# First batch's queries in runs of 256, 128 and 384 tokens, and cluster products of both halves in one run

## The chip, the cores and the metric

The kernel runs on one core of one Trainium2 chip. The metric is the device time of one execution in microseconds (us); the time of a kernel is the median of its runs. A profile is one further execution, taken by the hardware profiler. Engines are named as the profile names them: PE (matrix products), PEld (its weight loads, which run beside the products), DVE (vector), ACT (activation functions), POOL and SP. SP computes nothing here; it issues DMAs. POOL casts, and issues DMAs on a software queue. Each engine works through its own instructions in order.

## The reference

Each query and key is given to the cluster of its head whose normalised centroid it fits best; a query attends only to keys of its own cluster. The result goes, token by token, through a gated feed forward.

```python
q_assign = np.argmax(np.einsum('bhsd,hcd->bhsc', q_n, c_n), axis=-1)
k_assign = np.argmax(np.einsum('bhsd,hcd->bhsc', k_n, c_n), axis=-1)
mask = q_assign[:, :, :, None] == k_assign[:, :, None, :]
scores = np.where(mask, scale * np.matmul(q, k.transpose(0, 1, 3, 2)), -1000000000.0)
attn = softmax(scores)                      # over the keys
x = (attn @ v).transpose(0, 2, 1, 3).reshape(B * S, H * D)
out = (1 / (1 + np.exp(-(x @ w_gate))) * (x @ w_val)) @ w_out
```

There are B = 4 batches, H = 8 heads, S = 768 tokens, D = 64; 16 clusters for each head; w_gate and w_val are 512 x 1536, w_out is 1536 x 512.

## The kernel before, in words

**Tiles.** Heads are worked in four pairs p = 0 to 3; `even` and `odd` hold the keys and queries of one pair for the even and the odd tokens, cast to 16 bits, with 16 more rows that mark the cluster ("mask rows"), so that one product gives score and mask at once. For the first batch the mask rows of `even` and of most of `odd` are made by DVE (L506, called from `place`, L675); the rows of the odd queries come by a DMA, `odd<-even` (L693). A block is (batch, half of the tokens qb, pair p) with 384 queries. `attend` (L905) works two of a block's 12 units (head of the pair, 128 keys) at a time: two score products of 384 columns into one `sc` buffer (L921), one exponential over both, 768 columns, into `es` (L939), six value products of 65 columns from `es` (L967). After the twelfth unit DVE divides by the sums (L1005, L1008), and the block is turned into the columns of `x`, by a DMA transpose on SP (L1031) or, where that would be late, by PE and a DVE copy (L1016, L1027): in the before, for pairs 2 and 3 of the first half of batch 0, and for the last block.

**Feed forward.** `feed` (L1055) starts when all four pairs of a half are in `x`: for each of 12 chunks of the hidden layer four gate products and four value products of 384 columns (L1066), a tanh on ACT (L1082), a gated product on DVE (L1093) into `hT`. Then for each 128 tokens three runs of four output products of 512 columns (L1113), a copy by ACT (L1128) and a DMA of 256 KB to the output.

**Preparation.** Pairs of batch 0 are prepared by `prepare_first` and `prepare_pair` (PE transposes L824 and L716, cluster products L870 and L756). Later batches are prepared two pairs at a time by `prepare` (L511): for batch 1's pairs 0 and 1 PE transposes (L546), later DVE transposes (L527) of keys and queries that came in as quarters (16 DMAs of 96 KB for two pairs, L410); then cluster products in 32 bits, four for each half of the rows, each half into a `ring` buffer of its own (L614 to L619); then four to five DVE instructions for each half (L481 to L506) and eight small DMAs for the mask rows.

**Buffers.** In the products' memory: `sc` twice, `av` once, `ring` three times. `es` four times.

**Order.** All of it is laid out by a planner written into the kernel (`Order`, L38). Each piece of work is a task with an engine, a duration in us written by hand (0.73 for an exponential, 0.165 for a score product), its predecessors, the buffers it takes, and a due time (`due_at`, L268, by the block's place; `due_ffn`, L271, by the work of the feed forward). It plays the engines forward and gives each free engine the ready task that is due first; what it finds is only the order, and the order is emitted. On the chip the engines then run in that order, held up by semaphores alone. The blocks of batch 0 stand in the order (qb, p) = (0,0), (1,0), (0,1), (0,2), (0,3), (1,1), (1,2), (1,3) (L255 to L258), so the first feed forward comes after five blocks.

Of the kernel before, what the change touches and what calls it, by code (L numbers as in the profile page):

```python
# [9 lines left out]
FP = mybir.dt.float32  # L10
# [161 lines left out]
def kernel(  # L172
# [82 lines left out]
    blocks = [(b, qb, p) for b in range(B) for qb in range(2) for p in range(NP)]  # L255

    for at, of in ((1, 4),):
        blocks.insert(at, blocks.pop(of))  # L258
    JS = list(range(0, NCH, 2)) + list(range(1, NCH, 2))
    units = []  # L260
    for b, qb, p in blocks:
        js = [(e, j) for e in range(2) for j in JS]
        units += [(b, qb, 2 * p + e, j) for e, j in js]
    NS = len(units)
    NB = 12 * 2 * NP
    S1, T1 = 60, 36.0

    def due_at(slot):  # L268
        return T1 + (slot - S1) * (0.42 if slot < S1 else 0.78)

    def due_ffn(work):  # L271
        return T1 + work * 1.8
# [8 lines left out]
    def dma(eng, out_of, in_of, size, deps=(), due=0.0, acq=(), uses=(), early=0.0, seq=(), pkt=65, lat=0.0):  # L281
        return od.add(
            eng, 0.69 if pkt == 13 else ISSUE[eng], lambda: Q[eng].dma_start(out=out_of(), in_=in_of()),
            deps, due, acq=acq, uses=uses, dma=size, early=early, lat=lat, seq=seq, pkt=pkt,
        )
# [74 lines left out]
    c4 = od.add("DVE", 1.0, c_scale, [c2], due=-8.8)  # L360
# [16 lines left out]
    c_cblk = od.add("DVE", 0.5, c_place, [c5, c_small], due=-4, uses=[c_ring])  # L377
# [9 lines left out]
    def load_nat(b, p, nm, eng, due, early=0.0, hold=None, behind=()):  # L387
        src = {"k": k, "q": q, "v": v}[nm]
        buf = natb[b, p, nm] = Buf("nat")
        if isinstance(due, tuple):  # L390

            nat[b, p, nm] = []
            for e in range(2):
# [5 lines left out]
                        0.6, (), due[e], acq=[] if e else [buf], uses=[buf] if e else [],  # L399
# [111 lines left out]
    def prepare(b, grp, due, step, act=(), queues=("SP",), split=False):  # L511
# [97 lines left out]
        turned = []  # L609
        for half in range(2):  # L610
            cols = slice(half * QB, (half + 1) * QB)
            rg, t1, mx, oh = (Buf(x) for x in ("ring", "t1", "mx", "oh"))

            def scored(cols=cols, rg=rg, half=half):  # L614
                ps = take(rg)
                for g, (p, nm) in enumerate(sides):
                    nc.tensor.matmul(  # L617
                        out=ps[32 * g : 32 * g + 32, :QB], lhsT=cblk[:, 2 * p + half, :],
                        rhs=t32[p, nm].tile[:, cols], start=True, stop=True,  # L619
                    )  # L620
# [12 lines left out]
            cl = od.add(  # L633
                "PE", 0.85, scored, [cp[p, nm, half] for p, nm in sides] + [c_cblk], due,
                lat=0.3, acq=[rg], uses=[t32[x] for x in sides],
            )
            a1 = od.add(
                "DVE", 0.53, lambda t1=t1, rg=rg: turn_scores(take(t1)[:n], rg.tile[:n, :QB]),
# [61 lines left out]
    def prepare_pair(b, p, due, step, act=("q",), direct=False):  # L700
# [63 lines left out]
        def same():  # L764
# [7 lines left out]
            "PE", 0.85, scored, [*cp.values(), c_cblk], due, lat=0.3, acq=[rg],  # L772
# [10 lines left out]
        if direct:  # L783
            place(
                b, p, oh, tiles, last, due + (5 if p == 1 else 0.0), [c["k", 0], c["k", 1]],
# [20 lines left out]
    def prepare_first(due):  # L806
# [8 lines left out]
        for nm, h in (("k", 0), ("k", 1), ("q", 0), ("q", 1)):  # L815
# [19 lines left out]
            def cast(e, nm=nm, cols=cols):  # L835
# [8 lines left out]
                "PE", 0.65, turn, [nat[0, 0, nm][h], c_ident], due, lat=0.3, seq=turns[-1:],  # L844
# [30 lines left out]
        def same():  # L875
# [3 lines left out]
            "PE", 1.0, scored, [*cp.values(), c_cblk], due, lat=0.3, acq=[rg],  # L879
# [25 lines left out]
    def attend(slot):  # L905
# [3 lines left out]
        b, qb, h, _ = units[slot]  # L909
        p = h // 2  # L910
        two = [(u[2] % 2, u[3]) for u in units[slot : slot + 2]]
        qb_ = aug[b, p][qb]
        sc, es = Buf("sc"), Buf("es")
        vp = vps[(b * NP + p) % NVP]
        t1 = []
        for i, (e, j) in enumerate(two):
            kb = aug[b, p][j % 2]

            def score(i=i, e=e, j=j, kb=kb):
                ps = sc.tile if i else take(sc)  # L920
                nc.tensor.matmul(  # L921
                    out=ps[:, i, :QB],
                    lhsT=kb.tile[0:80, 0, e * QB + j // 2 * 128 : e * QB + (j // 2 + 1) * 128],
                    rhs=qb_.tile[0:80, 1, e * QB : (e + 1) * QB],
# [5 lines left out]
                    "PE", 0.165, score,  # L930
                    masked[b, p, j % 2, "k", e] + masked[b, p, qb, "q", e],
                    due - (20.0 if slot < S1 else 0.0), lat=0.25,
# [4 lines left out]
            scored_last.append(t1[-1])  # L937
        def exponentials():
            i = nc.scalar.activation(  # L939
                take(es), sc.tile[:, :, :QB], AF.Exp, bias=nbias,  # L940
# [12 lines left out]
        n = slot % (2 * NCH)  # L953
        first, last = n == 0, n == 2 * NCH - 2
        if first:
            avb[b, qb, p] = Buf("av")
        av = avb[b, qb, p]
# [3 lines left out]
        def value():  # L961
            if first:
                take(av)
            for i, (e, j) in enumerate(two):
                for c in range(QCH):
# [3 lines left out]
                        lhsT=es.tile[:, i, c * 128 : (c + 1) * 128], rhs=vp[:, e, j, :],  # L969
                        start=first and i == 0 and c == 0, stop=last and i == 1 and c == QCH - 1,  # L970
                    )

        def value_and_zeros():
            value()

            for _ in range(2):
                nc.tensor.matmul(
                    out=av.tile[:, : 2 * QCH * (D + 1)].rearrange(
                        "p (c e d) -> p c e d", e=2, d=D + 1
                    )[:, :, two[1][0]],  # L980
# [13 lines left out]
        for e, _ in two:  # L994
            last_av[b * NP + p, e] = [t3]
        if not last:
            return
# [234 lines left out]
```

## Time and profile before

| | us |
|---|---|
| median of 3 runs (325.75, 325.77, 326.37) | 325.77 |
| the profiled execution's own time | 325.53 |
| its span, first to last instruction | 323.8 |
| PE busy | 315.7 |
| ACT busy | 228.6 |
| DVE busy | 147.1 |
| POOL busy | 64.7 |

The span is 1.7 us shorter than the time of the same execution; what lies around it is the start and the end of the launch. Busy means that at least one instruction of the engine is under way. A product counts as busy from its start to the end of its pass through the array, and several overlap: a PE that is 98% busy can still have stood still between two starts. How far apart products start when nothing holds them up, their pitch, is read from the timeline.

### The profile page before, as it was taken

What the parts mean: (1) busy time and instruction counts of PE and PEld (TensorE: products, weight loads), DVE (VectorE), ACT (ScalarE), POOL (GpSimd) and SP (SyncE); (2) the same over time, 40 slices, a digit from 0 to 9 for tenths busy, and PEclk for the clock granted to TensorE, in tenths of its full rate; (3) what the DMA queues carried; (4) which work ended last, traced back from release to release, by engine and by line L of the source; (5) the groups of instructions that cost most, each with busy time, mean ns of one, the idle gap of its engine ahead of it and who ended that gap; (6) DMA issues with size and microseconds to landing.
All of it is one profiled execution on the core that took longest, in us unless ns stands there. A gap on an engine that the chain in (4) does not pass through costs nothing.

```text
span 323.8 us, 7113 instructions
## 1 busy us (share of the span) xinstructions
PE 315.7 (98%) x2811; PEld 186.1 (57%) x2811; DVE 147.1 (45%) x336; ACT 228.6 (71%) x329; POOL 64.7 (20%) x105
## 2 busy tenths in 40 slices
PE   7999999999999999999999999999999999999995
PEld 3566556654666556565566556565566655655652
DVE  3899733356536266751147563832023310530430
ACT  5899868866698768686888678687788877323331
POOL 4997613131004403300013423100000000000000
PEclk9999999999999999999999999999999999999999
DMA  7999999672566896312667865410210012002002
GB/s 237 359 161 263 226 246 238 107 140 70 115 98 126 183 183 147 90 38 62 136 97 145 165 127 141 126 43 9 79 47 12 14 45 79 1 2 97 0 3 97
DMA packets 91522, 36.87 MB, mean 114 GB/s; under 512 B 76961, under 2 KB 86689, under 8 KB 91489
## 3 DMA queue, kind: packets, MB, share of 16 engines
q1 hardware_dynamic: 84960, 26.56, 36.6%
q0 software_dynamic: 6096, 9.44, 14.2%
q10 hardware_dynamic: 432, 0.43, 0.5%
q8 instruction: 22, 0.36, 0.5%
q14 instruction: 12, 0.09, 0.1%
HBM read 28.34 MB, written 6.29 MB: 107 GB/s over the span
## 4 chain that ended last, share of the span: by engine, by line
PE 93%; ACT 3%; DMA 1%; DVE 1%; issue 0%
PE ring L1066 39%; PE ring L1113 19%; PE sc L921 18%; PE av L967 10%; PE ring L617 3%; ACT es L939 3%; DMA odd<-even 1%; PE ring L546 1%; PE av L307 1%; PE ring L824 1%; DVE even L506 0%; PE ring L870 0%; PE ring L716 0%; ACT t L833 0%; DVE ohf L495 0%; PE ring L756 0%
## 5 line engine op out<-in xcount | busy, mean ns | idle before, releaser
L939 ACT ACTIVATE es<-sc,nbias 128x768 f16<-128x768 f32 x192 | 170.4, 901 | 38.1 <-PE sc L921 36.8
L1093 DVE SCALAR_TENSOR_TENSOR hT<-gt,ring 128x384 f16<-128x384 f32 x96 | 53.1, 553 | 106.0 <-PE ring L1066 97.6
L1066 PE MATMUL ring<-x,wv 128*128 128x384 f16 x384 | 78.2, 326 | 0.0
L1066 PE MATMUL ring<-x,wg 128*128 128x384 f16 x384 | 78.1, 325 | 0.0
L967 PEld LDWEIGHTS <-es 128*128 128x128 f16 x1152 | 56.5, 97 | 29.4 <-ACT es L939 7.7
L1113 PE MATMUL ring<-wo,hT 128*128 128x512 f16 x288 | 71.1, 379 | 0.0
L1082 ACT ACTIVATE gt<-ring 128x384 f32<-128x384 f32 x96 | 46.9, 488 | 34.1 <-DVE hT L1093 18.9
L967 PE MATMUL av<-vp,es 128*128 128x65 f16 x1152 | 64.5, 193 | 0.4 <-ACT es L939 0.3
L1066 PEld LDWEIGHTS <-wv 128*128 128x128 f16 x384 | 35.3, 97 | 21.1
L1066 PEld LDWEIGHTS <-wg 128*128 128x128 f16 x384 | 35.0, 97 | 20.7
L579 POOL CAST even<-t 128x768 f16<-128x768 f32 x24 | 19.9, 830 | 115.2 <-DVE t L527 93.0
L1113 PEld LDWEIGHTS <-hT 128*128 128x128 f16 x288 | 25.1, 98 | 23.6 <-issue 1.2
L921 PE MATMUL sc<-even 80*128 80x384 f16 x96 | 25.8, 326 | 1.4 <-DVE even L506 0.7
L921 PE MATMUL sc<-odd,even 80*128 80x384 f16 x96 | 26.2, 326 | 0.7 <-ACT es L939 0.4
L921 PEld LDWEIGHTS <-even 80*128 80x128 f16 x192 | 17.3, 98 | 16.2 <-issue 3.0
L921 PE MATMUL sc<-odd 80*128 80x384 f16 x96 | 26.2, 325 | 0.1
L921 PE MATMUL sc<-even,odd 80*128 80x384 f16 x96 | 26.1, 325 | 0.1
L1128 ACT ACTIVATE osb<-ring 128x512 f32<-128x512 f32 x24 | 14.3, 597 | 16.2 <-PE ring L1113 14.5
L921 PEld LDWEIGHTS <-odd 80*128 80x128 f16 x192 | 16.8, 99 | 12.9 <-issue 3.2
L1005 DVE RECIPROCAL rr<-av 128x6 f32<-128x6 f32 x32 | 6.1, 191 | 36.9 <-PE av L967 36.8
L527 DVE STREAM_TRANSPOSE t<-nat 128x384 f32<-128x384 f32 x40 | 20.6, 552 | 2.9 <-DMA nat<-in_q_dram 2.4
L453 POOL CAST vp<-nat 128x384 f16<-128x384 f32 x32 | 16.0, 532 | 19.2 <-DMA nat<-in_v_dram 19.0
(72 smaller groups left out, 157.3 us busy)
## 6 DMA issues: line engine op xcount, KB each, us to landing
out_dram<-osb SPq DMA_DIRECT2D x24, 256.0 KB, 2.1
nat<-in_v_dram POOLq DMA_DIRECT2D x12, 384.0 KB, 5.1
nat<-in_k_dram SPq DMA_DIRECT2D x40, 96.0 KB, 3.3
nat<-in_q_dram SPq DMA_DIRECT2D x40, 96.0 KB, 3.2
odd<-even SPq DMA_DIRECT2D x12, 192.0 KB, 3.4
nat<-in_k_dram SPq DMA_DIRECT2D x5, 384.0 KB, 5.6
nat<-in_q_dram SPq DMA_DIRECT2D x5, 384.0 KB, 6.2
nat<-in_v_dram SPq DMA_DIRECT2D x4, 384.0 KB, 7.2
```

Of the source, the lines that this page charges most:

```text
L453: lambda e=e: nc.gpsimd.tensor_copy(vps[i % NVP][:, e, :, 0:D], buf.tile[:, e, :, :]),
L527: nc.vector.transpose(t[:, half * QB : (half + 1) * QB].rearrange("p (c x) -> p c x", x=128), blocks_[:, half],)
L579: nc.gpsimd.tensor_copy(t[:, NM[nm], cols], t32[p, nm].tile[:, cols])
L617: nc.tensor.matmul(out=ps[32 * g : 32 * g + 32, :QB], lhsT=cblk[:, 2 * p + half, :], rhs=t32[p, nm].tile[:, cols], start=True, stop=True,)
L921: nc.tensor.matmul(out=ps[:, i, :QB], lhsT=kb.tile[0:80, 0, e * QB + j // 2 * 128 : e * QB + (j // 2 + 1) * 128], rhs=qb_.tile[0:80, 1, e ...
L939: i = nc.scalar.activation(take(es), sc.tile[:, :, :QB], AF.Exp, bias=nbias, scale=D ** -0.5 if quarters(b, p) else scale,).ins
L967: nc.tensor.matmul(out=av.tile[:, g : g + D + 1], lhsT=es.tile[:, i, c * 128 : (c + 1) * 128], rhs=vp[:, e, j, :], start=first and i == 0 ...
L1066: nc.tensor.matmul(out=ps[:, :QB], lhsT=ws[fc // FPG][:, dcc, fc % FPG, :], rhs=xb.tile[:, dcc, :], start=(dcc == 0), stop=(dcc == NDC - 1),)
L1082: lambda rg=rg, gt=gt: nc.scalar.activation(take(gt), rg.tile[:, :QB], AF.Tanh, scale=0.5),
L1093: nc.vector.scalar_tensor_tensor(t[:, fc, :], gt.tile, 1.0, rv.tile[:, :QB], ALU.add, ALU.mult)
L1113: nc.tensor.matmul(out=ps, lhsT=hb.tile[:, fc, tb * 128 : (tb + 1) * 128], rhs=wos[fc // FPG][:, fc % FPG, :], start=(fc == 0), stop=(fc = ...
L1128: "ACT", 0.5, lambda rg=rg, osb=osb: nc.scalar.mul(take(osb), rg.tile, 0.5),
```

## The change

1. **Blocks of batch 0.** The first half is split into a part of 256 tokens and one of 128; the second half stays whole (384). The 256 tokens of all four pairs are a group of their own, with one feed forward of 256 columns; the other 128 and the 384 make a second group, with a feed forward of 512 columns. Batches 1 to 3 keep two groups of 384. The order of batch 0 is: 256 of pair 0, 384 of pair 0, 256 of pairs 1, 2, 3, and then 128 of pair 0, and 128 and 384 of pairs 1, 2, 3.
2. **Units together.** `attend` takes as many units as fill the score buffer: four of 256 columns (an exponential of 1024), six of 128 (768), two of 384 (768, as before).
3. **Cluster products of later batches** of both halves stand in one run of eight, in the two banks of one `sc` buffer in place of two `ring` buffers.
4. **Queues and the end.** Batch 1's quarters for pairs 2 and 3 (16 DMAs) are issued by POOL, no longer by SP. The first load of pair 1's keys waits for the centroids' sum on DVE. The last 128 tokens' output is made as 384 columns and then 128, each with its own copy and DMA.
5. **Numbers of the planner**: durations, due times, the weights' load times.

```diff
-        "es": ([128, 2, QB], HP), "rr": ([128, 2 * QCH], FP),
-        "xn": ([128, QCH, 128], HP), "x": ([128, NDC, QB], HP), "hT": ([128, NFC, QB], HP),
-        "gt": ([128, QB], FP), "osb": ([128, DM], FP),
+        "es": ([128, 1024], HP), "rr": ([128, 2 * QCH], FP),
+        "xn": ([128, QCH, 128], HP), "x": ([128, NDC, 512], HP), "hT": ([128, NFC, 512], HP),
+        "gt": ([128, 512], FP), "osb": ([128, DM], FP),
...
+    SPLIT = ((0, 0, 2), (0, 2, 1), (1, 0, 3))
+    groups = {(0, 0): SPLIT[:1], (0, 1): SPLIT[1:]}
...
+    blocks = [
+        (0, 0, 0, SPLIT[0]), (0, 1, 0, SPLIT[2]), (0, 0, 1, SPLIT[0]), (0, 0, 2, SPLIT[0]),
+        (0, 0, 3, SPLIT[0]),
+    ]
+    blocks += [
+        (0, 1, p, part) for p in range(NP) for part in SPLIT[1:] if (p, part) != (0, SPLIT[2])
+    ]
...
-    S1, T1 = 60, 36.0
+    S1, T1 = 96, 51.1
...
-        return T1 + (slot - S1) * (0.42 if slot < S1 else 0.78)
+        return T1 + (slot - S1) * (0.442 if slot < S1 else 0.78)
...
+        rg = Buf("sc")
+
+        def scored():
+            ps = take(rg)
+            for half in range(2):
+                for g, (p, nm) in enumerate(sides):
+                    nc.tensor.matmul(
+                        out=ps[32 * g : 32 * g + 32, half, :QB], lhsT=cblk[:, 2 * p + half, :],
+                        rhs=t32[p, nm].tile[:, half * QB : (half + 1) * QB], start=True, stop=True,
+                    )
+
+        cl = od.add(
+            "PE", 1.45, scored, [cp[p, nm, half] for p, nm in sides for half in range(2)] + [c_cblk],
+            due, lat=0.3, acq=[rg], uses=[t32[x] for x in sides],
+        )
...
-            cl = od.add(
-                "PE", 0.85, scored, [cp[p, nm, half] for p, nm in sides] + [c_cblk], due,
-                lat=0.3, acq=[rg], uses=[t32[x] for x in sides],
-            )
...
+        b, gr, p, (par, c0, nq) = block
+        N = 128 * nq
+        together = 1024 // N if nq != QCH and 512 % N == 0 and 12 % (1024 // N) == 0 else 768 // N
+        per = together // 2
...
-                take(es), sc.tile[:, :, :QB], AF.Exp, bias=nbias,
+                take(es)[:, : together * N].rearrange("p (u c) -> p u c", u=2),
+                sc.tile[:, :, : per * N], AF.Exp, bias=nbias,
...
-            "ACT", 0.73, exponentials,
+            "ACT", 0.13 + 0.00078 * together * N, exponentials,
...
-        if not ((b, qb) == (0, 0) and p >= 2 or slot >= NS - 2):
+        if not ((b, gr) == (0, 0) and p >= 2 or block == blocks[-1]):
...
+        pieces = [(tb, chunk, 0, DM) for tb, chunk in enumerate(chunks)]
+        if (b, gr) == (B - 1, 1):
+            tb, chunk, _, _ = pieces.pop()
+            pieces += [(tb, chunk, 0, 384), (tb, chunk, 384, 512)]
...
-            0, p_, "k", "SP", -8 + p_, hold=ones if p_ == 1 else None,
+            0, p_, "k", "SP", -8 + p_, hold=[c1] if p_ == 1 else None,
...
-                            b + 1, p_, nm, "SP", max(due - 40, 20),
-                            due - 60 if b else 42 if grp[0] else 20,
+                            b + 1, p_, nm, "POOL" if (b, grp[0]) == (0, 2) else "SP", max(due - 36.0, 20),
+                            due - 60 if b else 42 if grp[0] else 17.5,
```

In the order that the planner makes of it, counted from the first score product: the first feed-forward product comes after 88 score products (48 of 256 columns, 16 of 384, 24 of 128), 144 value products, 16 runs of three transposes and three runs of cluster products; before the change after 70 score products of 384 columns, 204 value products, 16 runs of three transposes and five runs of cluster products. Between each of the six runs of eight cluster products and the next product that takes the same `sc` buffer there stand at least two score products, one run of value products and one run of four feed-forward products. The two DVE instructions that free that buffer (L490 of the changed kernel, the transposes L481 of before) stand directly behind each other in five of the six cases.

More of the change, by code (lines that the diff above doesn't have):

```diff
@@ L359 @@
     )
-    c4 = od.add("DVE", 1.0, c_scale, [c2], due=-8.8)
+    c4 = od.add("DVE", 1.2, c_scale, [c2], due=-8.8)
     c_ring = Buf("av")
@@ L375, in c_place @@
             )
[L377 removed]
+    c_cblk = od.add("DVE", 0.6, c_place, [c5, c_small], due=-4, uses=[c_ring])
     nat, natb = {}, {}
@@ L963, in value @@
                 take(av)
-            for i, (e, j) in enumerate(two):
-                for c in range(QCH):
+            for i, (e, j) in enumerate(some):
+                for c in range(nq):
                     g = (2 * c + e) * (D + 1)
@@ L1053, in attend, with feed @@
         )
-    def feed(b, qb, work):
-        xb, hb = x_of[b, qb], Buf("hT")
+        return together
+    def feed(b, gr, work):
+        xb, hb = x_of[b, gr], Buf("hT")
+        nt = sum(part[2] for part in groups[b, gr])
+        N, w = 128 * nt, nt / 3
         done = []
@@ L1164 @@
     done = {}
-    for b, qb, p in blocks:
-        if (qb, p) == (0, 0) and b + 1 < B:
+    for block in blocks:
+        b, gr, p, part = block
+        if (gr, p) == (0, 0) and b + 1 < B:
             for grp in ((0, 1), (2, 3)):
```

205 lines of the change are left out of this document (102 added, 103 removed).

## The prediction

> **What bounds the kernel now.** The page first, then the chain of waits, then busy time by stretch, then PE's and ACT's timelines where PE stands still.
>
> ```profile
> PE 315.7 (98%) x2811; PEld 186.1 (57%) x2811; DVE 147.1 (45%) x336; ACT 228.6 (71%) x329; POOL 64.7 (20%) x105
> PEclk9999999999999999999999999999999999999999
> PE 93%; ACT 3%; DMA 1%; DVE 1%; issue 0%
> ```
>
> PE carries the chain, at full clock. So the time is PE's work plus the moments in which PE stands still, and the change leaves the columns to multiply as they are. The question is where PE stands still, and a pipelined engine hides that in "busy". I take pitches from undisturbed runs in the timeline: six feed-forward runs of four products from 43.33 to 47.23 us, 0.1625 us a product; score products the same; value products 0.031; three transposes 0.36. A cluster run:
>
> ```profile
> 34.92 0.49 PE L921 MATMUL sc<-even,odd 80*128 80x384 f16 x2
> 35.34 0.85 PE L617 MATMUL ring<-t,cblk 128*32 128x384 f32 x8
> 36.12 0.66 PE L921 MATMUL sc<-even 80*128 80x384 f16 x3
> ```
>
> Two score products from 34.92 end their turn at 35.25; the run starts 0.09 later and the next product follows 0.78 after that: 0.87.
>
> Stage A runs from the first score product (11.31) to the first feed-forward product (43.33), 32.0 us. Its work: 70 score products 11.4, 204 value products 6.3, 16 transposes of three 5.8, five cluster runs 4.35, the rest 0.3: 28.1. **PE stands still for 3.9 us.** Stage B, to the first output product at 66.10, lasts 22.8; its work is 96 x 0.1625 + 28 x 0.163 + 84 x 0.031 = 22.8: no stall. After it the same pitches hold in every stretch that I looked at. All that can be won from overlap lies in stage A.
>
> ```profile
> 11.30:43.30 32.00, 29.98 (x368) 19.67 (x369) 27.46 (x66) 29.89 (x39) 25.12 (x36) 1.00 1.15 237
> 43.30:66.10 22.80, 22.80 (x214) 14.57 (x212) 8.05 (x16) 17.12 (x26) 3.56 (x7) 1.00 1.02 190
> ```
>
> (Window; length; busy PE, PEld, DVE, ACT, POOL; clock; DMA share; GB/s.) ACT is busy for 29.89 of 32 us in stage A: ACT sets the pace there, PE waits for it.
>
> ```profile
> 11.83 5.05 ACT L939 ACTIVATE es<-sc,nbias 128x768 f16<-128x768 f32 x6 [1.38 <-PE sc L921]
> 17.35 0.90 ACT L939 ACTIVATE es<-sc,nbias 128x768 f16<-128x768 f32 x1 [0.47 <-PE sc L921]
> ...
> 22.32 14.03 ACT L939 ACTIVATE es<-sc,nbias 128x768 f16<-128x768 f32 x17
> ```
>
> Seventeen exponentials in 14.03 with the last one's 0.90: a pitch of 0.82, 0.80 where nothing is between. The gap before 17.35 is the wait for the odd queries' mask rows:
>
> ```profile
> 12.39 4.38 DMA odd<-even
> ```
>
> That DMA stands behind the loads of batch 0 and lands at 16.77.
>
> **Stage A after.** PE's work by the new counts: 48 score products of 256 columns at 0.109 (between 0.1625 and the 0.055 of the 128-column row below) 5.2, 24 of 128 at 0.055 1.3, 16 of 384 2.6, 144 value products 4.5, transposes 5.8, three cluster runs 2.6, rest 0.2: 22.2. ACT's side: an exponential of 1024 columns is not in the trace. By proportion to 768 it has a pitch of 1.07; two output copies of 512 (L1128, pitch 0.49 in the trace) would be 0.99. I take 1.05, nearer to the row of the same operation. The first three end at about 15.5 with one copy of 0.37 (L723); then the block of 384 needs the odd queries' rows, whose DMA has the same loads ahead of it, so ACT starts again at 17.35 as before, having waited 1.9 in place of 0.5. The held key load, waiting for DVE's sum at 3.8 instead of 2.1, moves little: q's two loads use the path meanwhile (bounds -0.4 and +0.5). Then 6 x 0.80 + 3 copies x 0.37 = 5.9, to 23.3; nine of 1024 9.45, to 32.7; DVE's mask rows for pair 3, ready at 28.98 before and at about 29 by the new order, are just in time. The first feed-forward product stands in PE's order behind a score pair that needs a buffer freed by the third exponential after that: 35.1. From there PE runs a pair 0.33, the last turn 0.11, 12 value products 0.37, a pair, a transpose: it starts at 36.8. That is 25.5 us for 22.2 of work: 3.3 us of stall against 3.9. **Term: -0.6**, bounds -2.4 (stall 1.5, ACT kept fed) and +0.8.
>
> **Stage B after.** 96 x 0.109 + 32 x 0.163 + 24 x 0.055 + 144 x 0.031 + one run of eight cluster products 1.6: 23.1 us on PE. ACT: 20 exponentials 16.0 and 12 tanh at 0.27 (0.39 pitch at 384) 3.2: 19.2. PE is the bound by 3.9 us. Term 0.
>
> **Cluster runs.** Within a run the second pass starts 0.35 after the first; a run of eight should cost 0.09 + 3 x 0.35 + 0.44 = 1.57 against 2 x 0.87. Six times 0.17 to 0.18: **-1.1**, bounds -1.3 and 0. It needs the `sc` buffer freed in time: two DVE transposes, 0.51 apart, free it 1.35 after the run; the planned products between are worth 1.55 to 2.2. Where DVE is late that cover is gone, and each 0.2 of lateness eats one run's gain. Below zero only if DVE is over 0.4 late each time.
>
> **The end.**
>
> ```profile
> 317.63 2.54 PE L1113 MATMUL ring<-wo,hT 128*128 128x512 f16 x11
> ...
> 320.21 0.60 ACT L1128 ACTIVATE osb<-ring 128x512 f32<-128x512 f32 x1 [1.99 <-PE ring L1113]
> ```
>
> After the last product: copy 0.60, DMA of 256 KB 2.1. A copy of 128 columns lies between 0.20 (the 128x1 activations) and 0.49 (384); by the step from 384 to 512 (0.11) it is 0.27, 0.33 less. A DMA of 64 KB is between 1.9 (24 KB) and 2.1: 0 to 0.2 less. **-0.4**, bounds -0.5 and 0.
>
> **Narrow products.** 48 score products more (432 for 384), 12 output products of 128 columns. The nearest row:
>
> ```profile
> L1016 PE MATMUL ring<-ident,xn 128*128 128x128 f16 x9 | 1.0, 219 | 0.0
> ```
>
> Three of these with a weight load each span 0.33, of which 0.22 is the last one's pass: 0.055 apart; the value products with 65 columns are at 0.031. Weights are loaded behind the products, so I add 0.1 in all, within rounding. The Trainium skill ("TensorE: Matmul & The Clock Gate", section "Back-to-back issue gap") speaks against the change here: it gives about 81 ns for each pair of weight load and product of 128 columns in a sustained stream, by which 60 such products would cost some 1.6 us more. The trace's 55 ns speaks against that, on nine products.
>
> **Queues.** SP loses 16 issues of 0.65 and gains four transposes of 1.2 (33 for 29). POOL gains 16 issues; its DMAs take 0.70 to 0.88 each, and behind them stand the casts of the next three v tiles, used some 10 us later. Cost 0 as long as the transfers land in time (second rival).
>
> **Sum:** 325.53 - 0.6 - 1.1 - 0.4 = 323.4; the median of the runs lies 0.24 above the profiled execution: **323.7 us**.
>
> **Rivals.**
> (1) *Stage A pays more* (0.17). ACT stays fed, 1024 columns cost 0.99, the stall falls to 1.5: -2.4 - 1.1 - 0.5, 321.7 or so. For it: feed-forward work is there 6.5 us sooner. Against: ACT's share, and the wait at 17.35.
> (2) *Slower: batch 1's quarters come late* (0.20). They now queue behind the feed forward's weights, whose last one landed at 54.13 before; two v loads came by 56.95. SP's 16 landed from 56.74 to 70.93, 0.95 apart, two transposes' issues of 1.2 among them; 0.79 without these. From 57 at 0.79 the 16th lands at 69.6. DVE transposes them (L527) in order between the gated products of the 512-column feed forward; by PE's count these turns come at about 66.0, 67.7, 69.4 and 71.3, for quarters 7, 10, 13 and 16, due at 62.5, 64.9, 67.3, 69.6. DVE is in order, so a late quarter holds the gated products, and with three `ring` buffers PE stops within 1 us. It decides from 0.89 us a quarter; at 1.15 the last is 4.1 late and the kernel is at about 327.5, a few tenths being hidden by the buffers. For it: nothing in the trace issues such quarters from POOL. Against: with 128-byte pieces SP's took 66% of the DMA engines in that stretch, so there is room. The Trainium skill ("SBUF — State Buffer", section "SBUF: two separate sides") says that POOL cannot write descriptors while DVE holds the port they share; that would favour this rival, and the even 0.70 to 0.88 of POOL's issues does not show it.
> (3) *A hand-over stalls* (0.16). The last block's transpose has 5.2 us of output products to hide 4 us, the mask rows of batch 1 land about 1 us ahead of need; if either is late by 1.3 us: 325.0.
> (4) *Narrow products cost more* (0.05): if the weight load's own 0.097 (PEld) set the pitch, 60 x 0.042 = 2.5, of which the 24 in stage A hide 1.0: +1.5, 325.2.
> The forecast has 0.42.
>
> **How the numbers follow.** A measurement of this kernel tells about 0.2% (0.65 us) from no change. Faster: forecast 0.42, (1) 0.17 and 0.09 of (3), 0.68. Same: the other 0.07 of (3) and (4), 0.12. Slower: 0.20. The range takes in (1) and a mild (2): 321.4 to 327.2.
>
> **What would show it.** First exponential after the wait at 17.3 to 17.6; pitch of 1024 columns 1.05; first feed-forward product near 36.8; no PE gap from there to 62; cluster runs 1.57; last copy 0.27. It is wrong if DVE waits for `nat` between 63 and 72 us, or if PE waits on `sc` behind cluster runs.

## The result, and the profile after

The changed kernel takes 324.42 us (median of its 22 executions) beside 325.81 for the kernel before in the same rounds; the ratio is 0.9955, 95% interval 0.9938 to 0.9971. The forecast was 323.7, range 321.4 to 327.2. One of the 22 executions, of 659.09 us, counts as slow, as do the two highest of e2 below, and no ratio holds them.

The median hides two groups. Each run lists the clock that PE (TensorE) was granted over the whole run: fourteen runs at 0.999 to 1.0 took 323.43 to 324.69, median 323.86; seven at 0.995 took 325.42 to 326.48, median 325.64. Nothing lies between them. So the forecast's time is that of two thirds of the executions, and a third pays 1.8 us that no step of the prediction had.

The kernel before is not free of the lower clock either. This measurement lists no clocks for it (325.5 to 326.74, and two executions at 327.32 and 328.0). In the rounds of the experiments, which do list them, 10 of its 67 executions are at 0.995: seven took 326.25 to 326.57, within half a microsecond of its full-clock median (325.9 to 326.2), and three 327.97 to 328.21. Where its clock falls, no trace shows.

The profiled execution, 325.91 us, is of the upper group. Its page, the lines that answer to the three shown of before:

```profile
PE 315.6 (97%) x2869; PEld 193.0 (60%) x2869; DVE 147.0 (45%) x344; ACT 224.6 (69%) x326; POOL 76.2 (24%) x121
...
PEclk9979999999999999999999999999999999999999
...
PE 90%; ACT 4%; DMA 3%; DVE 1%; issue 1%; SPq 0%; ACTq 0%
```

The clock row has a 7 in its third slice, 16 to 24 us, where before it had only nines. The same by stretch: first stage A (first score product 10.71, first feed-forward product 39.05), then three pieces of 2 us, then the 3.4 us up to 17.92:

```profile
10.71:39.05 28.34, 25.25 (x309) 18.77 (x310) 22.55 (x59) 22.76 (x27) 23.30 (x35) 0.94 1.10 257
16.00:18.00 2.00, 0.35 (x3) 0.18 (x3) 1.88 (x6) 0.49 (x1) 2.00 (x4) 0.98 1.10 342
18.00:20.00 2.00, 1.99 (x7) 1.06 (x6) 0.19 (x1) 1.15 (x2) 1.94 (x3) 0.50 1.22 210
20.00:22.00 2.00, 2.00 (x18) 0.65 (x18) 0.42 (x1) 0.95 (x3) 1.92 (x4) 0.67 1.23 199
14.50:17.92 3.42, 1.63 (x25) 1.16 (x23) 3.17 (x9) 1.51 (x3) 3.37 (x7) 1.00 1.08 358
```

PE is busy for 0.35 us of the two before 18, then "busy" all the time with few products, at a clock of 0.50. A mean of 0.67 from 20 to 22 means half clock until about 21.3; 0.98 from 16 to 18 means that it began at 17.9. In the 3.4 us up to there PE was busy for 1.63, less than half. What stands ahead of it, on PE and on ACT:

```profile
18.02 1.12 PE L938 MATMUL sc<-odd,even 80*128 80x384 f16 x3 [1.66 <-DMA odd<-even]
```
```profile
18.85 1.69 ACT L957 ACTIVATE es<-sc,nbias 128x768 f16<-128x768 f32 x2 [1.92 <-PE sc L938]
```

The line of before for the same wait, the one for the odd queries' mask rows:

```profile
16.82 0.50 PE L921 MATMUL sc<-odd,even 80*128 80x384 f16 x2 [0.33 <-DMA odd<-even]
```

So this wait, 0.33 us on PE before, is 1.66 now, and behind it PE runs at half clock for 3.4 us. ACT starts its fourth exponential at 18.85; the forecast had 17.35.

The changed kernel was run once more later (e13, below), and there the profile caught an execution of the lower group, 323.84 us. It is the one to hold against the forecast:

```profile
10.74:36.94 26.20, 23.53 (x309) 18.40 (x310) 22.48 (x59) 22.59 (x27) 22.70 (x33) 1.00 1.19 271
36.94:60.62 23.68, 23.48 (x314) 18.59 (x312) 9.36 (x27) 20.72 (x34) 13.69 (x20) 1.00 1.13 215
```
```profile
17.44 0.65 PE L938 MATMUL sc<-odd,even 80*128 80x384 f16 x3 [1.45 <-DMA odd<-even]
```

The wait is nearly as long, 1.45 us, the clock stays full, and the first feed-forward product comes at 36.94; forecast 36.8. Of the 2.1 us by which that of the upper execution is later (39.05), 0.6 is the later landing of its rows (17.97 and 17.39) and 1.5 lies behind it, with the half clock. A cluster run of eight in the same execution, between its neighbours, and the end:

```profile
56.79 0.60 PE L1081 MATMUL ring<-x,wg 128*128 128x256 f16 x4
57.32 1.50 PE L625 MATMUL sc<-t,cblk 128*32 128x384 f32 x16
58.75 0.61 PE L1081 MATMUL ring<-x,wv 128*128 128x256 f16 x4
```
```profile
318.34 0.49 ACT L1153 ACTIVATE osb<-ring 128x384 f32<-128x384 f32 x1 [1.35 <-PE ring L1136]
319.06 0.28 ACT L1153 ACTIVATE osb<-ring 128x128 f32<-128x128 f32 x1 [0.23 <-PE ring L1136]
```

The four products from 56.79 end their turn at 57.22 (four pitches of 0.1085), the next product starts at 58.75: 1.52 for the run, with two of 0.87 before. From the last copy to the end of the span it is 322.0 - 319.06 = 2.94, before 323.8 - 320.21 = 3.59.

So at full clock, against the profiled execution of before (325.53); 0.16 of the measured terms' sum is not in the difference of the times:

| term | forecast | measured | from |
|---|---|---|---|
| stage A | -0.6 | -0.5 | 36.94 less 22.2 of work, 14.7; before 43.33 - 28.1 = 15.2 |
| stage B | 0 | +0.6 | 23.68 long, 23.1 of work |
| cluster runs | -1.1 | -1.3 | 6 x (1.74 - 1.52) |
| end | -0.4 | -0.65 | 2.94 for 3.59 |
| sum | -2.1 | -1.85 | 323.84 - 325.53 = -1.69 |

### The profile page after: what moved, and what is told of

Its sections match the earlier page's. It is cut to its first block, busy times and chain, and to the rows that moved or that the text cites. A ratio compares the mean times of both kernels' runs of the same rounds, so it can differ in the third digit from the quotient of the medians.

```text
span 324.1 us, 7275 instructions
## 1 busy us (share of the span) xinstructions
PE 315.6 (97%) x2869; PEld 193.0 (60%) x2869; DVE 147.0 (45%) x344; ACT 224.6 (69%) x326; POOL 76.2 (24%) x121
## 2 busy tenths in 40 slices
DMA packets 80273, 36.94 MB, mean 114 GB/s; under 512 B 65072, under 2 KB 75056, under 8 KB 80240
## 3 DMA queue, kind: packets, MB, share of 16 engines
q0 software_dynamic: 6864, 11.01, 17.2%
## 4 chain that ended last, share of the span: by engine, by line
PE 90%; ACT 4%; DMA 3%; DVE 1%; issue 1%; SPq 0%; ACTq 0%
PE ring L1081 38%; PE ring L1136 19%; PE sc L938 18%; PE av L985 10%; ACT es L957 4%; PE sc L625 3%; DMA odd<-even 2%; DMA nat<-in_k_dram 1%; DVE even L515 0%; PE ring L769 0%; PE ring L555 0%; PE ring L884 0%; PE ring L837 0%; DVE ohf L504 0%; PE ring L729 0%
## 5 line engine op out<-in xcount | busy, mean ns | idle before, releaser
L957 ACT ACTIVATE es<-sc,nbias 128x768 f16<-128x768 f32 (+1 forms) x188 | 166.5, 918 | 34.8 <-PE sc L938 33.1
L1108 DVE SCALAR_TENSOR_TENSOR hT<-gt,ring 128x384 f16<-128x384 f32 (+2 forms) x96 | 53.1, 553 | 99.9 <-PE ring L1081 97.4
L1081 PE MATMUL ring<-x,wv 128*128 128x384 f16 (+2 forms) x384 | 78.1, 326 | 0.0
L1081 PE MATMUL ring<-x,wg 128*128 128x384 f16 (+2 forms) x384 | 78.1, 325 | 0.0
L1097 ACT ACTIVATE gt<-ring 128x384 f32<-128x384 f32 (+2 forms) x96 | 47.1, 490 | 32.6 <-DVE hT L1108 16.8
L1136 PE MATMUL ring<-wo,hT 128*128 128x512 f16 (+2 forms) x300 | 69.5, 370 | 0.0
L985 PEld LDWEIGHTS <-es 128*128 128x128 f16 x1152 | 54.9, 97 | 20.7 <-ACT es L957 0.5
L1153 ACT ACTIVATE osb<-ring 128x512 f32<-128x512 f32 (+2 forms) x25 | 14.5, 580 | 24.7 <-PE ring L1136 24.6
L938 PEld LDWEIGHTS <-even 80*128 80x128 f16 x216 | 19.5, 98 | 15.2 <-issue 6.2
L938 PE MATMUL sc<-even 80*128 80x384 f16 (+2 forms) x120 | 26.5, 294 | 1.1 <-POOL even L757 0.6
L938 PE MATMUL sc<-even,odd 80*128 80x384 f16 (+2 forms) x120 | 26.2, 293 | 0.0
L1010 DVE RECIPROCAL rr<-av 128x6 f32<-128x6 f32 (+2 forms) x36 | 6.8, 190 | 36.9 <-PE av L985 36.7
L462 POOL CAST vp<-nat 128x384 f16<-128x384 f32 x32 | 15.9, 538 | 15.2 <-PE av L985 7.8
```

The lines of the kernel that those rows point to most:

```text
L462: lambda e=e: nc.gpsimd.tensor_copy(vps[i % NVP][:, e, :, 0:D], buf.tile[:, e, :, :]),
L938: nc.tensor.matmul(out=ps[:, i // per, i % per * N : (i % per + 1) * N], lhsT=kb.tile[0:80, 0, e * QB + j // 2 * 128 : e * QB + (j // 2 + ...
L957: i = nc.scalar.activation(take(es)[:, : together * N].rearrange("p (u c) -> p u c", u=2), sc.tile[:, :, : per * N], AF.Exp, bias=nbias, s ...
L985: nc.tensor.matmul(out=av.tile[:, g : g + D + 1], lhsT=es.tile[:, i * N + c * 128 : i * N + (c + 1) * 128], rhs=vp[:, e, j, :], start=firs ...
L1081: nc.tensor.matmul(out=ps[:, :N], lhsT=ws[fc // FPG][:, dcc, fc % FPG, :], rhs=xb.tile[:, dcc, :N], start=(dcc == 0), stop=(dcc == NDC - 1),)
L1097: lambda rg=rg, gt=gt: nc.scalar.activation(take(gt)[:, :N], rg.tile[:, :N], AF.Tanh, scale=0.5),
```

## The experiments

All ratios are to the kernel before in the same rounds, so that chips may differ. Where not said otherwise, an experiment keeps the order of the instructions on every engine. The edits are shown shortened: `...` stands for what is left out, and long lines are written out over several.

### First: is it the wait, and does it work through the clock?

**e1**, the held load undone:
```diff
-            0, p_, "k", "SP", -8 + p_, hold=[c1] if p_ == 1 else None,
+            0, p_, "k", "SP", -8 + p_, hold=ones if p_ == 1 else None,
```


> The changed kernel with one edit undone: the first load of pair 1's keys waits for the memsets again, not for the centroids' sum. The order on every engine is that of the changed kernel, save one memset. Theory T (the held load pushes every load behind it, and with them the DMA of the odd queries' mask rows, back by about 1.2 us; PE then stands still for 1.66 us at 16.4, and in about a third of the executions its clock falls to half for 3.4 us, which costs some 1.8 us): the rows land near 16.8, PE's wait shrinks to about 0.5 us, the clock stays full in every execution, and the times are one group around 323.3 us (half of the 1.2 us is won, the rest was hidden), none near 325.7. Rival R1 (the clock falls because products of 256 columns and short bursts leave PE less busy all through 8 to 26 us): two groups as before, 323.9 and 325.7. Rival R2 (the wait is hidden behind ACT's or POOL's work anyway): the rows land earlier, and the group of full clock stays at 323.9.

Measured: 323.89 us, ratio 0.9924 (0.9904 to 0.9944), six executions from 323.41 to 324.21, all at a clock of 0.999 to 1.0. PE's wait is 0.45 us:

```profile
17.51 0.65 PE L938 MATMUL sc<-odd,even 80*128 80x384 f16 x3 [0.45 <-DMA odd<-even]
```

One group, as theory T says; but its time is that of the full-clock group, not 0.5 less.

**e2**, the held load alone in the kernel before (the same line).

> The kernel before with the held load alone: the first load of pair 1's keys waits for the centroids' sum. The order on every engine is that of the kernel before, save one memset. Theory T: the odd queries' rows land 1.0 to 1.2 us later than 16.77, PE's wait there grows from 0.33 to about 1.4 us, and the time from 325.8 to between 326.3 and 326.9; if a wait of that length is enough for the clock to fall, part of the executions lie 1.8 us higher still. Rival R1: no execution shows a lower clock, as no product is narrower than before. Rival R2: 325.8, no change.

Measured: 328.12, ratio 1.0058 (1.0032 to 1.0084), twelve executions spread from 326.58 to 333.17. One edit of one wait makes the kernel before slower by 1.8 us by the medians (328.12 and 326.28). Two executions list a clock of 0.998 (326.58, 326.73), six 0.993 to 0.995 (327.77 to 329.01), and those above lower ones. A stretch of 3.4 us at half clock costs 1.7 us of 325, which is 0.005 in this mean (an estimate from the trace above), so the spread goes with one, two and more such stretches. The profile caught the lowest execution, at full clock, with the wait in it:

```profile
17.86 0.50 PE L921 MATMUL sc<-odd,even 80*128 80x384 f16 x2 [1.97 <-DMA odd<-even]
```

and PE's busy time, third number, in the 3.41 us that hold most of this wait:

```profile
16.25:19.66 3.41, 1.80 (x23) 1.32 (x27) 2.27 (x6) 1.30 (x4) 2.99 (x5) 1.00 1.15 176
```

**e3**, the odd rows' DMA issued by ACT:
```diff
-            "SP", lambda: od_.tile[64:80, NM["q"], :], lambda: ev.tile[80:96, NM["q"], :], 0.1,
+            "SP", 0.62, lambda: (nc.sync if p else nc.scalar).dma_start(...),
```


> The changed kernel with the DMA of pair 0's odd rows issued by ACT, between the first two exponentials of 1024 columns, no longer by SP behind the loads; the order on the other engines is that of the changed kernel. Theory T: on a queue of its own it lands some 2 us after its issue, near 15.5, PE does not wait for it at 16.4, the clock stays full, and ACT starts its fourth exponential near 16.9 in place of 18.85; ACT pays 0.65 us for the issue. Time one group, 322.4 to 323.2. Rival R1: the DMA lands early, and the clock still falls in a third of the executions. Rival R2 (DMA engines are busy with the loads, and the rows land no earlier than 17): 324 with the wait in place.

Measured: 323.89, ratio 0.9942 (0.9921 to 0.9962); six executions at 323.62 to 324.15, three at 325.30 to 325.43. ACT's issue and PE's wait:

```profile
11.82 0.60 ACTq L707 DMA_DIRECT2D odd<-even  x1
```
```profile
17.27 0.65 PE L938 MATMUL sc<-odd,even 80*128 80x384 f16 x3 [1.30 <-DMA odd<-even]
```

Issued at 11.82 on a queue of its own, 24 KB take until 17.2. Seven loads of 384 KB are then under way on SP's queue, landing from 11.98 to 18.34, 1.06 apart. In the trace none of the rows' packets moves before 15.9; the rows land ahead of the last two loads (17.36 and 18.34) and behind the other five. Rival R2 has it: another queue gains next to nothing, and 1.30 us of waiting still brings the second group: the three list a clock of 0.995, the six 0.999 to 1.0.

**e4**, PE kept busy in the wait:
```diff
                 ps = sc.tile if i else take(sc)
+                for _ in range(7 if block == blocks[1] and at + i == 0 else 0):
+                    nc.tensor.matmul(out=ps[:, 1], lhsT=wz[:, 0:128], rhs=wz, start=True, stop=True)
```


> The changed kernel with seven products of zeros, 512 columns each (1.5 us), put into PE's order right ahead of the score product that waits for the odd rows, in the bank that this product then overwrites. They leave the wait as it is and only keep PE busy in it. Theory T with the clock as its second part: the rows still land near 17.97, the clock stays full in every execution, and all times lie around 323.9. Rival R1: the clock still falls in a third of the executions, 325.7. If the fall needs no idle PE at all, nothing changes; if the wait alone made the second group, without the clock, it stays too.

Measured: 324.06, ratio 0.9931 (0.9911 to 0.9951), six executions from 323.77 to 324.47. The wait is filled and nothing else moves:

```profile
15.82 1.67 PE L937 MATMUL sc<-wz 128*128 128x512 f16 x7
17.47 0.65 PE L938 MATMUL sc<-odd,even 80*128 80x384 f16 x3
```

**e10**, the same in e2, eight products in its wait.

> The kernel before with the held load (as e2) and eight products of zeros, 512 columns each (1.7 us), ahead of the score product that waits 1.97 us for the odd rows there. Theory (an idle PE of that length lets its clock fall in most executions of e2; the wait itself costs only the 1.05 us by which the rows land later): one group near 326.8 to 327.1, and the executions of 328 and more are gone. Rival (e2's spread came from the loads or from something else that PE's idle time has no part in): 328 with the same spread.

Measured: 326.37, ratio 1.0014 (1.0000 to 1.0028), eleven of twelve executions from 326.02 to 326.69 at a clock of 0.998 to 1.0, the twelfth at 328.26 and 0.995; the kernel before in these rounds has two of 29 at 0.995. By the medians, work that computes nothing makes e2 1.75 us faster (on two chips, on which the kernel before took 326.28 and 326.25). That is below what was expected, too: in the order of before the later landing itself costs at most a few tenths by the medians, 0.8 at the first feed-forward product of the trace.

**e13**, the changed kernel again.

> The changed kernel once more, on the chip of the three others. Theory (clock): two groups again, near 323.9 and, in about a third, 325.6 (or the whole of it shifted with the kernel before on this chip). Rival (the upper group belonged to the chip of the first measurement): one group.

Measured: 324.07, ratio 0.9957 (0.9940 to 0.9974); seven executions at 323.44 to 324.11 and a clock of 0.998 to 1.0, five at 325.09 to 326.00 and 0.995. Two groups on this chip too.

What follows: with the idle PE in place, 12 of 33 executions of the changed kernel and 3 of 9 of e3 lie in the upper group; with the wait short (e1) or filled (e4) none of 12 does. If a third were the true share there as well, none of 12 would happen about once in 130 times; e5, e8 and e9 below, whose wait is short or gone, add 22 executions with none. That the idle PE brings the clock down is shown by these, by e2 and e10, and by the trace of the one execution that has it. The products of 256 columns (R1) are in all of them. That the executions without a trace which lie high are there through the clock is shown by the clocks that they list: 0.995 for all 15. What brings the clock of the kernel before down, in 10 of 67 executions, stays open.

But theory T is wrong in its other half. It had the landing delayed by 1.2 us and half of that won back in e1. Over all the traces the last load of batch 0 (ten of 384 KB behind pair 0's; the expectations' 13 is a miscount) lands at 16.6 to 17.3 without the hold (six) and at 16.9 to 17.8 with it (eight): 0.4 on average, and the profiled execution was a late one. In exchange pair 0's second load of queries lands at 5.0 to 5.4 in place of 6.2 to 6.7, and in the new order the first exponential starts at 11.7 to 12.1 in place of 12.3 to 12.8. Everything after the wait hangs on the landing alone:

| | rows land | first feed-forward product | difference |
|---|---|---|---|
| before, e2, e10 | 16.77, 17.82, 17.57 | 43.33, 44.36, 44.11 | 26.56, 26.54, 26.54 |
| e1, e3, e4, e13 | 17.47, 17.23, 17.43, 17.39 | 36.99, 36.77, 36.97, 36.94 | 19.52, 19.54, 19.54, 19.55 |

The hold wins about 0.8 us ahead of the wait (the means of these two ranges of traces are 11.78 and 12.56) and loses it in the wait. That led to the next pair.

### Second: what if the rows don't come by a DMA?

**e8**, the held load undone, and the rows of the odd queries of pair 0 made by two more transposes on DVE, as those of the odd keys are:
```diff
-        m = dma(
-            "SP", lambda: od_.tile[64:80, NM["q"], :], lambda: ev.tile[80:96, NM["q"], :], 0.1,
...
+        if p == 0:
+            for h in range(2):
+                g = tiles.index(("q", h))
+                turn_matches(od_.tile[64:96, NM["q"], h * QB : (h + 1) * QB], ohf.tile[32 * g : 32 * g + 32, 32 : 32 + QB])
```


> The changed kernel with the held load undone (as e1), and pair 0's odd query rows made by two more DVE transposes in place of the DMA, so that they no longer stand behind 13 loads. Theory W (what starts ACT again is only the landing of these rows, and each us there is a us at the first feed-forward product, 36.97 in e4, and at the end): the rows are there by 14, ACT's fourth exponential starts at 17.0 to 17.5 in place of 18.03, the first feed-forward product by 36.0 to 36.5, time 323.2 +- 0.3. Rival (DVE pays: 0.77 us more on an engine that is busy nearly all the time there, and the copies and mask rows of pair 1 behind it are late by as much): 323.9 or more, with ACT waiting for PE later on, between 18 and 24 us.

**e9**, the same with the held load.

> As e8, with the held load as the changed kernel has it. Theory W: the held load lets pair 0's second load of queries land 1.2 to 1.5 us sooner and the first exponential start 0.7 to 1.0 sooner (11.7 for 12.8); with the DMA it was lost again in the wait for the odd rows, without it it is kept: fourth exponential at 16.2 to 16.8, first feed-forward product by 35.3 to 35.8, time 322.5 +- 0.4, one group at full clock as PE never stands still over a us after 10. Rival (DVE pays): 323.5 or more.

Measured: e8 323.85, ratio 0.9929 (0.9914 to 0.9944), no better than e1. e9 **322.84, ratio 0.9900 (0.9886 to 0.9915)**, four executions from 322.73 to 323.32: the fastest version of this study. ACT in e8:

```profile
12.51 1.11 ACT L957 ACTIVATE es<-sc,nbias 128x1024 f16<-128x1024 f32 x1 [1.81 <-PE sc L938]
...
17.56 0.49 ACT L736 ACTIVATE t<-ring 128x384 f32<-128x384 f32 x1 [1.61 <-PE ring L729]
17.95 1.69 ACT L957 ACTIVATE es<-sc,nbias 128x768 f16<-128x768 f32 x2
```

and in e9:

```profile
11.70 1.11 ACT L957 ACTIVATE es<-sc,nbias 128x1024 f16<-128x1024 f32 x1 [1.62 <-PE sc L938]
...
16.39 0.49 ACT L736 ACTIVATE t<-ring 128x384 f32<-128x384 f32 x1 [1.25 <-PE ring L729]
16.78 1.69 ACT L957 ACTIVATE es<-sc,nbias 128x768 f16<-128x768 f32 x2
```

In e8 the rows are in time, and the fourth exponential starts at 17.95, where e1 had 18.03: ACT now waits for PE's transposes of pair 3 (L729); these wait 0.50 us for DVE's copies of pair 2 to free their `ring` buffer, and DVE has 0.77 us more to do. Theory W failed there and DVE, the rival, was late next. In e9 the first exponential starts 0.8 sooner, the one at 16.78 and the feed forward at 35.76 1.2 sooner (e8: 17.95 and 36.92), both as W had them; between the two, one DVE instruction (L504) lasts 0.92 us in e8 and 0.56 in e9. The held load is worth 1.0 us (e9 against e8) as soon as nothing behind the loads holds the block of 384.

### Third: the other parts alone

**e5**, e1 with the cluster products in two runs of four again (the diff of the change, backwards, for `prepare`). The planner makes a new order of it.

> The changed kernel with the held load undone (as e1) and the joined cluster products undone too: two runs of four in ring buffers of their own. Theory (the joined run is worth its saved entries and exits, and nothing behind it is late): six times 0.2, so 1.2 to 1.3 us more than e1's 323.9, 325.1 to 325.2; cluster runs of 0.87 in the trace. Rival (the gain was given back, since the sc buffer is freed later than a ring buffer would be): within 0.3 of e1.

Measured: 325.57, ratio 0.9986 (0.9975 to 0.9996), 1.7 us above e1 by the medians and by the traces from the first feed-forward product on (323.2 - 36.41 against 322.1 - 36.99). PE is busy for 10.2 us with these products in e5 and 9.0 in e1. That is 1.2, near the 1.3 measured above; the other 0.5 is put down to the other order, which is argued and not shown.

**e7**, e1 with batch 1's quarters issued by SP, at the places in SP's order that they had in POOL's:
```diff
-            lambda: Q[eng].dma_start(out=out_of(), in_=in_of()),
+            lambda: Q["SP" if pkt == 13 else eng].dma_start(out=out_of(), in_=in_of()),
```


> The changed kernel with the held load undone (as e1) and batch 1's quarters for pairs 2 and 3 issued by SP again; the order on the engines is that of the changed kernel, the 16 loads stand in SP's order where they stood in POOL's. Theory (the queue makes no difference, as the transfers land ahead of need from either): within 0.3 of e1's 323.9. Rival (they or the transposes behind them on SP come late; that is what the move to POOL was worth): 324.5 or more, with DVE waiting for nat, or PE for x, between 62 and 75 us.

Measured: 328.87, ratio 1.0094 (1.0065 to 1.0123), 5 us above e1. SP's issues, PE, and the stretch of PE's wait and what follows:

```profile
66.36 2.04 SPq L292 DMA_DIRECT2D nat<-in_q_dram  x3
68.52 1.31 SPq L1043 DMA_TRANSPOSE x<-xn  x1
...
71.29 0.58 PE L1081 MATMUL ring<-x,wg 128*128 128x512 f16 x1 [4.89 <-DMA x<-xn]
```
```profile
70.01:76.84 6.83, 5.55 (x14) 1.92 (x14) 1.64 (x3) 1.19 (x2) 0.83 (x1) 0.50 0.26 69
```

The quarters themselves are in time. The transpose that completes `x` for the second group stands behind them on SP, is issued at 68.52, lands at 71.25, and PE waits 4.89 us for it. That is what the move to POOL takes out of the way. But the 5 us are not this wait alone. All six executions list a lower clock, 0.989 to 0.995; the profiled one (331.48, 0.989) is the highest, and in its trace PE runs at half clock from 70.01 to 76.84. Of the 7.5 us between its span and e1's (329.6 and 322.1), the wait is 4.9, and half clock from 71.29 to 76.84 makes about 2.8 (an estimate, half of that stretch). How much is clock in the other five, these runs don't part. And a planner told of SP's load would have put the quarters elsewhere, so 5 us is the price of this order, not of the queue as such.

**e11**, the kernel before with parts 3 (joined cluster runs) and the divided last output, and nothing else; the planner's order is new.

> The kernel before with the joined cluster products and the divided last output alone: blocks, unit groups, queues and the held load are those of before. By the traces the joined runs are worth 1.3 us and the end 0.7, and the blocks' gain of 0.5 in stage A is given back by 0.7 in stage B (theory G): 323.6 to 323.9 by the before of the first measurement (325.8), no worse than the changed kernel at full clock (323.86). Rival (the blocks are worth what was forecast, 0.6): 324.4 or more. If the merge needs the new order to be hidden, 325 or more.

Measured: 326.12, ratio 1.0009 (0.9996 to 1.0022). No gain: theory G falls. That the merge needs the new order fits this, but is argued. The trace shows one thing that may be a part of it. Behind a joined run at 81.84 PE waits for DVE:

```profile
90.83 0.81 PE L1070 MATMUL ring<-x,wg 128*128 128x384 f16 x4 [0.67 <-DVE hT L1097]
```
```profile
88.43 0.54 DVE L488 TENSOR_REDUCE mx<-t 128x24 f32<-128x384 f32 x1
89.01 0.56 DVE L495 TENSOR_TENSOR oh<-t,mx 128x384 f16<-128x384 f32 x1
89.60 0.32 DVE L634 TENSOR_SCALAR oh<-oh,weight 128x384 f16<-128x384 f16 x1
89.96 0.38 DVE L506 STREAM_TRANSPOSE oht<-oh 128x192 f32<-128x192 f32 x1
90.26 0.98 DVE L1097 SCALAR_TENSOR_TENSOR hT<-gt,ring 128x384 f16<-128x384 f32 x2
```

Both halves' scores arrive at once, the second half's mask work stands in DVE's order ahead of two gated products, and PE runs out of `ring` buffers. The other part in that trace, a first exponential at 12.92 (before: 11.83), begins with transposes that take 0.87 us where they took 0.52, and a cluster run that takes 2.14 where it took 1.48: in this trace PE has its full clock only from 10.33 on, in that of before from 5.41. Whether the executions without a trace lose there too stays open. In e12 PE waits for DVE as long at the same place (0.67 at 90.02).

**e12**, e11 with the held load and DVE's rows (as e9).

> As e11, with the held load and with pair 0's odd query rows made by two more DVE transposes in place of the DMA (as e9). Theory G with W (the rows' landing starts ACT again there too, and each us of it is a us at the end): first exponential 0.6 earlier, wait of 0.47 at 17.35 gone, time 0.7 to 1.0 below e11, 322.8 or so, level with e9 (322.84). Rival (in the order of before DVE's later mask rows are the next to be late, with the two transposes more by 0.8): within 0.3 of e11, or above.

Measured: 324.70, ratio 0.9958 (0.9944 to 0.9972): 1.4 below e11, more than W said, and 1.9 above e9. The new blocks, with POOL's quarters and the order that the planner finds for them, are thus worth 1.9 us in the company of the other edits; what of it is the blocks and what the place of DVE's work, these runs don't part.

## Why the prediction was right, and where not

- **The sum.** -2.1 forecast; measured -1.95 between 325.81 and the full-clock median 323.86, and -1.4 between the medians of all. It was right to look for the gain in the cluster runs and the end, and to put nothing on the columns. That the sum comes so close is partly luck: the 0.6 of stage B that was not forecast is nearly made up by the cluster runs (0.2 more than forecast) and the end (0.25 more), and stage A has its gain from elsewhere.
- **Stage A, -0.6.** The first feed-forward product was forecast at 36.8 and came at 36.94, through errors that cancel: the number is luck. PE's stall did not shrink to the 3.3 us forecast: 26.20 long, 22.2 of work, 4.0 of stall, where before had 3.9. The stage ends sooner because its first score product comes 0.6 sooner (10.74 for 11.31), with the second load of queries that the held load lets through, which the prediction did not see. Without the held load (e1) the stall is near the forecast: 36.99 - 11.81 = 25.18, 3.0 of stall; there the stage starts later instead. On the way, ACT started again at 17.96 and not at 17.35; an exponential of 1024 columns has a pitch of 1.01 (the two from 13.03 last 2.12, the single one 1.11), not 1.05, so that the way from there to the feed forward was 19.0 us and not 19.45. The steps that the prediction lists behind 35.1 add up to 1.5, to 36.6, where it writes 36.8.
- **"The held key load moves little", bounds -0.4 and +0.5.** This is the step that failed. Its direct price was inside the bounds, 0.4 on the landing. What it also does is to lengthen the stretch in which PE stands still from 0.45 us (e1) to 1.3 to 1.66, and that has a price of its own, through the clock, in one execution of three. The sum had priced ACT's wait and never asked what PE does meanwhile. That is why the median of all runs is 324.42 and not 323.9.
- **Stage B, term 0.** It is 0.6 longer than its work, in small waits: 0.15 us on PE behind an exponential is the longest that the timelines of e1 and e4 show there. ACT has 20.7 us of work for 23.7, below PE's, but not evenly.
- **Cluster runs, 1.57.** 1.52 each: -1.3, the bound. "Where DVE is late that cover is gone" did not happen in the changed kernel, and happened in e11.
- **The end, -0.4.** The copy took 0.28 (forecast 0.27). The DMA of 64 KB took 1.6 us and not 1.9 to 2.1: the row of the 24 KB mask DMA was no lower bound for it.
- **Narrow products.** 128 columns with weights of their own stand 0.055 to 0.056 us apart, score and output products alike, on 48 and 12 of them. The 81 ns of the Trainium skill ("TensorE: Matmul & The Clock Gate", section "Back-to-back issue gap") is not seen here, and rival (4) with it.
- **Rival (2), POOL's quarters late.** They landed from 59.05 to 68.17 and PE waited for none of them. The prediction asked only what POOL pays. What SP would have paid in the new order, with four more transposes on it, was the larger number: 5 us (e7), lower clock and all.
- **Rival (3), a hand-over stalls.** In the profiled execution the first output products run from 62.73 to 67.91, and the second group's feed forward follows at once.
- **Rival (1)** needed ACT fed through the wait; e9 comes nearest to it, by taking the wait away, and gains 1.0 of the 2 us.

## What to carry to other kernels

When a wait on the busiest engine gets longer, price it twice: by what it delays, and by how long that engine stands still. Here the first was nothing and the second 1.8 us in a third of the executions, and 1.8 in the median of e2; with seven products of zeros in the wait none of six executions had it (e4), with eight one of twelve (e10), about the share that the kernel before has. When an engine is fed sooner, follow the chain to the next thing that comes late, and see whether that moved too: the held load won 0.8 us and gave it back at a DMA that stood behind the loads of the whole batch, and was worth 1.0 us once that DMA was gone. And what an edit is worth depends on the order around it: the same joined cluster runs were worth 1.2 to 1.7 us in one order, and in the other, with the divided last output, nothing.

## What the runs showed of the hardware

- PE's clock fell to half for 3.4 us (17.92 to 21.33) after 1.66 us of idleness, and in other executions it stayed full after 1.45 (e13) and 1.97 (e2). Every stretch between two changes of the clock in these traces is a whole number of times 3.41 us: full from 4.26 to 17.92 and half to 21.33 in the profiled execution of the changed kernel, half from 70.01 to 76.84 in e7. Counted in such steps from where the clock became full, PE was busy for 1.63 of the 3.41 us ahead of the fall, and for 1.80 (e2), 1.89 (e3) and 1.96 (e13) of those that hold the wait, or most of it, where the clock stayed full. So how long the wait is and where it falls among these steps both count; a border near half of a step is an estimate from these four traces. The Trainium skill ("TensorE: Matmul & The Clock Gate", Part 1, "The HAM clock gate") has a free-running window of 3413 ns. The trace agrees with that length. The Trainium skill (the same page, section "Why this matters for your kernels") has as a practical bound no idle gap over about 3 us. For this kernel the measurement says otherwise: half of that was enough in one execution of three.
- A DMA of 24 KB between tiles on ACT's queue landed 5.4 us after its issue, behind five of the seven loads that were under way on SP's queue; none of its packets moved for the first 4 us (e3). The Trainium skill ("DMA: Bandwidth & Descriptors", section "Queues, rings and completion order") has each DMA engine take turns between its queues by packets. By that one would expect the small DMA to pass more of the loads; why it did not stays open.
